# Attention ahead of two Strassen layers: half-row transposes in pairs, and scores copied to SBUF by the maximum

## The chip, the cores and the metric

The kernel runs on one core of a Trainium2 chip. The metric is the device time of one execution in microseconds (us), the median of several. A core has five engines with queues of their own: TensorE (PE, matrix products, with weight loads shown apart as PEld), VectorE (DVE), ScalarE (ACT), GpSimd (POOL) and SyncE (SP), which here issues nearly all DMAs. Each works through its instructions in the order in which the program issues them. PSUM, where TensorE writes, has eight banks of 512 f32 a partition; SBUF is the working memory. A DVE or ACT instruction can read PSUM, POOL reads SBUF alone.

## The reference

Attention with a threshold, for 8 batches and 8 heads of 576 positions and 64 features, all in f32:

```python
scores = scale * np.matmul(q, k.transpose(0, 1, 3, 2))      # scale = 1/8
thresh = np.max(scores, axis=-1, keepdims=True) - tau       # tau = 0.02
scores = np.where(scores >= thresh, scores, -1000000000.0)
scores = scores - np.max(scores, axis=-1, keepdims=True)
attn = np.exp(scores)
attn = attn / (np.sum(attn, axis=-1, keepdims=True) + 1e-09)
return np.matmul(attn, v).astype(np.float32)
```

The result, as 4608 rows of 512, goes through `h = np.maximum(x @ w_in, 0.0)` and `h * h @ w_out`, with a hidden width of 2048.

## The kernel before

The program has two parts. First attention, with the weights of the two layers loaded and prepared beside it; then the two layers as nested Strassen products (`hidden_layer`, `output_layer`), of which nothing is changed but the allocation of their two PSUM buffers.

Two heads make a pair, since two heads of 64 features fill 128 partitions. There are 32 pairs, and 4.5 blocks of 128 queries in each, so 144 *units* of 128 queries by 576 keys for two heads; the fifth unit of a pair is shared with the next. A *period* (`period`, L579) handles two units: A = 2p and B = 2p+1 begin, a and b of the period before are finished, and the values of period m = p-2 are computed. Periods run from -2 to 74. The order in which `period` calls the steps is the program order of every engine; the steps are under a manual schedule, so nothing reorders them.

The steps of a unit:

- `turn`, `turn_last` (L343, L365): q and k of a pair come from DMA with positions on partitions, and are transposed by TensorE, four blocks of 128x128 into one bank of a two-buffer pool; ScalarE copies them out, scaling q by 1/8. The last 64 queries and keys of both heads share one block; POOL copies those keys into block-diagonal tiles (`kdiag`, L376).
- `scores` (L405) multiplies 64x64 parts of q by 512 keys, four products at once on the four quarters of the array; `scores_rest` (L383) gives the last 64 keys of both heads in one 128x128 product with `kdiag`. A score tile has three banks, and there are two of them.
- `softmax` (L420) holds what follows: `top`, VectorE's maximum over both heads from PSUM (L431); `least`, the threshold, on VectorE (L434); `power`, ScalarE's exponential from PSUM (L439); `mask`, VectorE's comparison times the exponential with the row sum accumulated (L444), one per head; `over` on POOL adds 1e-9 (L450); `inverse` on VectorE (L453); `normal`, POOL's scaling by the inverse (L456), one per head.
- `fill` and `filled` (L493, L504) transpose the weights, 18 blocks of 128x128 per period in six fills (two of them in the unused middle of the score tiles, two in the banks of the values), and ScalarE copies each fill to SBUF (L508).
- `values` (L510) multiplies them by v in 64x64 products, 36 per period and 54 where a unit is shared; the result leaves with one of the fills and goes to DRAM by DMA (`give_x`, L537).

Beside this, 32 chunks of the layers' weights come in as 64-bit patterns and are converted in six steps (`convert1` to `convert6`, L198 to L241: two each on ScalarE, POOL and VectorE), one chunk a period from period 2 to 18 and from 33 to 49; two of these steps on VectorE (L225, L233) and all on POOL read only SBUF. Then 88 sums of 128x512 of them (`sums`, L243) and 12 sums of the first x (`prepare_x`, L762) run on POOL (L131, L134), up to three in a period.

Two VectorE instructions of the same form, the mask and the fifth conversion step, as they stand:

```python
nc.vector.scalar_tensor_tensor(                      # L444, of(j) in PSUM
    out=w[:, :, j, :], in0=of(j), scalar=thr[:, j : j + 1], in1=w[:, :, j, :],
    op0=ALU.is_ge, op1=ALU.mult, accum_out=sm[:, j : j + 1],
)
nc.vector.scalar_tensor_tensor(                      # L233, hi and a in SBUF
    out=hi, in0=hi, scalar=-(1 << 30), in1=a, op0=ALU.bitwise_and, op1=ALU.bitwise_or
)
```

Of the kernel before, what the change touches and what calls it, by code (L numbers as in the profile page):

```python
# [48 lines left out]
def kernel(  # L49
# [66 lines left out]
        out=qscale[:, :], in0=tau_c[:, :], scalar1=0.0, scalar2=SCALE, op0=ALU.is_ge, op1=ALU.mult  # L116
# [5 lines left out]

    kdiag = [sb.tile([P, P], FP32, tag=f"kdiag{i}") for i in range(3)]
    qdiag = [sb.tile([P, 2, P], FP32, tag=f"qdiag{i}") for i in range(2)]
    for t in kdiag:
        nc.gpsimd.memset(t[:, :], 0.0)
    for t in qdiag:
        nc.gpsimd.memset(t[:, :, :], 0.0)
# [114 lines left out]
    def sums(W, which, at, done):  # L243

        first = [at[a][b] for a in range(2) for b in range(2)]
        for op, o, x, y in which:
            for k_ in first:
                to = W[o, k_] if o == y else weight_tile(W, o, k_)
                yield op(nc.gpsimd, to[:, :], W[x, k_][:, :], W[y, k_][:, :])
        for m in OUTER:  # L250
            for op, o, x, y in which:
                to = W[m, o] if o == y else weight_tile(W, m, o)
                yield op(nc.gpsimd, to[:, :], W[m, x][:, :], W[m, y][:, :])
            done(m)
# [19 lines left out]
    SPARE = S  # L274
# [24 lines left out]
    def load_k(i):  # L299
# [4 lines left out]
        for j in range(2):  # L304
            queue = nc.scalar if i == 0 and j == 0 else nc.sync
            keys = k[b, h + j, :, :].rearrange("(p c) d -> p c d", c=CH)
            for e in range(2):
                queue.dma_start(
                    out=kn[ds(e * HALF, HALF), :, ds(j * D, D)],
                    in_=keys[:, j : j + CH - 1, :].rearrange("p (t e) d -> p t e d", e=2)[:, :, e, :],  # L310
                )
            queue.dma_start(out=rn[REST:P, ds(j * D, D)], in_=keys[:, 0 if j else CH - 1, :])
# [16 lines left out]
    def places(i):  # L329
        if i not in turned:  # L330
            turned[i] = (
                sb.tile([P, MAIN], FP32, tag="qT", bufs=2, name="qT"),
                sb.tile([P, S], FP32, tag="kT", bufs=3, name="kT"),
            )
# [8 lines left out]
    def turn(i, which):  # L343

        nat, to = loaded.pop((i, which)), places(i)[which]
        pt = bank([P, FULL, P], "pqk")
        for t in range(FULL):
            nc.tensor.transpose(pt[:, t, :], nat[:, t, :], ident[:, :])
        flat, to = pt[:, :, :].rearrange("p t m -> p (t m)"), to[:, 0:MAIN]

        def then():
            if which:
                nc.scalar.copy(to, flat)  # L353
                next_keys(i)
            else:
                nc.scalar.activation(out=to, in_=flat, func=AF.Identity, scale=qscale[:, :])
# [5 lines left out]
    def last_q(i):  # L362
        return qdiag[i // 2 % 2][:, i % 2, :]

    def turn_last(i, pt):  # L365

        rn = loaded.pop((i, 2))
        nc.tensor.transpose(pt, rn[:, :], ident[:, :])

        def then():  # L370
            to = last_q(i)[:, ds(i % 2 * REST, REST)]
            nc.scalar.activation(out=to, in_=pt[:, 0:REST], func=AF.Identity, scale=qscale[:, :])
            nc.scalar.copy(places(i)[1][:, MAIN:S], pt[:, REST:P])
            for j in range(2):
                rows = ds(j * D, D)
                nc.gpsimd.tensor_copy(out=kdiag[i % 3][rows, ds(j * REST, REST)], in_=turned[i][1][rows, MAIN:S])  # L376
# [4 lines left out]
    soft, given = {}, deque()  # L381

    def scores_rest(n, sc):  # L383

        pair, t = units[n]
        to = sc[:, MAIN:S]
        to = bass.AP(tensor=to.tensor, offset=to.offset, ap=[to.ap[0], [2 * BANK - S, 2], [1, REST]])
        if t < FULL:
            nc.tensor.matmul(to, turned[pair[0]][0][:, ts(t, P)], kdiag[pair[0] % 3][:, :], start=True, stop=True)
            return  # L390
        for c, i in enumerate(pair):
            nc.tensor.matmul(to, last_q(i)[:, :], kdiag[i % 3][:, :], start=(c == 0), stop=(c == 1))

    def apart(one, others):

        for o in others:
            tc.declare_no_dep(one.ins, o.ins, reason="other banks")

    mains, middles = {}, {}

    def aside(n, read):
        apart(read, mains.get(n, ()))
        middles.setdefault(n, []).append(read)

    def scores(n, sc):  # L405

        pair, t = units[n]
        mains[n] = []
        for c in range(2):
            for j in range(2):  # L410
                rows, at = ds(j * D, D), ds(c * HALF, HALF)
                qT, kT = turned[pair[c]]
                lhs = qT[rows, ds(t * P + c * HALF, HALF)] if t < FULL else last_q(pair[c])[rows, at]
                made = nc.tensor.matmul(sc[at, ds(j * 2 * BANK, MAIN)], lhs, kT[rows, 0:MAIN], start=True, stop=True)  # L414
                apart(made, middles.get(n, ()))
                mains[n].append(made)

    AT = (0, 2 * BANK - REST)

    def softmax(n, sc):  # L420

        small = sb.tile([P, 4, 2], FP32, tag="small", bufs=4, name="small")
        nmx, thr, sm, rs = (small[:, i, :] for i in range(4))
        both = sc[:, 0:S]
        both = bass.AP(tensor=both.tensor, offset=both.offset, ap=[both.ap[0], [AT[1], 2], [1, S]])
        w = sb.tile([P, CH, 2, D], FP32, tag="w", bufs=4, name="w")
        weights[n] = w
        of = lambda j: sc[:, ds(AT[j], S)].rearrange("p (c d) -> p c d", d=D)

        def top():  # L430
            nc.vector.tensor_reduce(out=nmx, in_=both, axis=AXIS.X, op=ALU.max, negate=True)  # L431

        def least():
            nc.vector.tensor_scalar(  # L434
                out=thr, in0=nmx, scalar1=-1.0, scalar2=tau_p[:, :], op0=ALU.mult, op1=ALU.subtract
            )

        def power(j):
            nc.scalar.activation(  # L439
                out=w[:, :, j, :], in_=of(j), func=AF.Exp, bias=nmx[:, j : j + 1], scale=1.0  # L440
            )

        def mask(j):
            nc.vector.scalar_tensor_tensor(  # L444
                out=w[:, :, j, :], in0=of(j), scalar=thr[:, j : j + 1], in1=w[:, :, j, :],
                op0=ALU.is_ge, op1=ALU.mult, accum_out=sm[:, j : j + 1],
# [30 lines left out]
    class Plan:  # L477


        def __init__(self, m):  # L480
            sizes = (2, 3, 3, 4, 3, 3) if turned_last(m + 2) else (1, 3, 3, 4, 4, 3)
            order = [(u, c) for u in range(2) for c in range(CH)]
            self.fills = [order[sum(sizes[0:f]) : sum(sizes[0 : f + 1])] for f in range(6)]
            self.first = [P if f < 2 else 0 for f in range(6)]
            self.size = [self.first[f] + P * n for f, n in enumerate(sizes)]
            self.base = [sum(self.size[0:f]) for f in range(6)]
            self.at = {
                uc: self.base[f] + self.first[f] + P * i for f, fill in enumerate(self.fills) for i, uc in enumerate(fill)
            }

    plans = {}

    def fill(m, f, pt):  # L493

        if m not in wT:
            wT[m] = sb.tile([P, 5 * BANK], FP32, tag="wT", bufs=1, name="wT")
            plans[m] = Plan(m)
        if has(2 * m):
            for i, (u, c) in enumerate(plans[m].fills[f]):
                w = weights[2 * m + u]  # L500
                to = pt[:, ds(plans[m].first[f] + P * i, P)]
                nc.tensor.transpose(to, w[:, c, :, :].rearrange("p j d -> p (j d)"), ident[:, :])  # L502

    def filled(m, f, pt, pv=False, copy=nc.scalar.copy):  # L504

        plan = plans[m]
        a, z = 0 if pv else plan.first[f], plan.size[f] if has(2 * m) else P
        return copy(wT[m][:, ds(plan.base[f] + a, z - a)], pt[:, a:z])  # L508

    def values(m):  # L510

        out = [bank([P, BANK], f"pv{j}") for j in range(2)]
        x = wT.pop(m)
        for c in range(CH):
            for u in range(2):
                for s, (i, _, count, row) in enumerate(halves(2 * m + u)):
                    for j in range(2):
                        rows = ds(j * D, D)
                        nc.tensor.matmul(  # L519
                            out[j][ds(u * D, D), ds(row, count)], loaded_v[i][rows, c, :],  # L520
                            x[rows, ds(plans[m].at[u, c] + row, count)],
                            start=(c == 0 and s == 0), stop=(c == CH - 1), skip_group_check=True,
                        )
        return out
# [12 lines left out]
    def give_x(m, x, step):  # L537

        for u in range(2):
            rows = ds(u * D, D)  # L540
            for i, first, count, row in halves(2 * m + u):
                b, hp = pairs[i]
                to = xT[b][ds(hp * P, P), ds(first, count)].rearrange("(j d) n -> d j n", j=2)
                of = x[rows, 0 : 2 * step].rearrange("p (j n) -> p j n", j=2)[:, :, ds(row, count)]
                given.append((to, of))
# [5 lines left out]
    OUT_SUMS = 15  # L551
    IN_FIRST = 33
    starts.update({IN_FIRST + m: 16 + m for m in range(16)})
    IN_SUMS = IN_FIRST + 13
    summing = deque()
# [14 lines left out]
    def sums_start(n):  # L570
        if n == OUT_SUMS:
            summing.append(sums(W_OUT, SUMS_B, AT_B, keep))
        if n == IN_SUMS:
            summing.append(sums(W_IN, SUMS_A, AT_A, lambda m: None))

    def begun(n):
        return starts.get(n)

    def period(p):  # L579
# [3 lines left out]
        sc = {}  # L583

        def first(f, pv):
            if has(2 * m) or has(2 * m + 2):
# [580 lines left out]
```

## Time and profile before

| what | us |
|---|---|
| median of three timed runs (1377.78 to 1378.17) | 1378.07 |
| span of the profiled execution, first to last instruction | 1379.4 |
| attention, about 13 to 580 us of the span | 567 |
| TensorE busy in the attention stage | 538 |
| VectorE busy there | 497 |
| ScalarE busy there | 469 |
| POOL busy there | 453 |
| the two layers, from 580 us on | 799 |

The page gives the profiled execution no time but its span. A line of a timeline has the start in us, the duration, the engine, the source line, the operation, what is written and read, and how many such instructions were merged; brackets hold the idle time in front and what ended it. A line of a group has the total busy time and the mean in ns, then the idle time in front of it. A line of a stretch gives its length, then busy us of PE, PEld, DVE, ACT and POOL with the number of instructions in brackets, then the granted TensorE clock as a share of full speed, the busy share of the DMA engines and GB/s. An f32 product shows as two instructions, a transpose as one. [...]

### The profile page before, as it was taken

How to read it: one execution, taken by the hardware profiler on the slowest of the kernel's cores; microseconds unless marked ns; L12 is line 12 of the kernel's file. 1: busy time of each engine (PE TensorE's matmuls, PEld its weight loads, DVE VectorE, ACT ScalarE, POOL GpSimd, SP SyncE). 2: the span in 40 equal slices, each digit the busy share in tenths (PEclk: the TensorE clock that was granted, in tenths of full speed). 3: DMA queues.
4: the chain of work that ended last, by engine and by line, in shares of the span. 5: the costliest groups of instructions: out<-in, count | busy, mean ns of one | idle time of the engine just before them, and what ended most of it. 6: DMA issues, size and time to landing. Idle time of an engine off the chain costs nothing.

```text
span 1379.4 us, 40958 instructions
## 1 busy us (share of the span) xinstructions
PE 1342.9 (97%) x15955; PEld 1185.5 (86%) x15955; DVE 1026.6 (74%) x2136; ACT 861.2 (62%) x1651; POOL 991.7 (72%) x1111
## 2 busy tenths in 40 slices
PE   8999999999999999999999999999999999999998
PEld 5676767666767676799999999999999999999998
DVE  5999988898998888677778777887666456654563
ACT  5999877888987777656766666765733224332330
POOL 2777888898888886355566556656877777777776
PEclk9999999999999999999999999999999999999999
DMA  4454325787432322123432343328962344224411
GB/s 116 129 144 131 93 71 158 215 231 217 135 89 66 75 66 56 36 90 123 151 125 88 106 146 131 110 106 325 386 209 66 116 154 154 85 79 145 154 32 31
DMA packets 200256, 177.26 MB, mean 129 GB/s; under 512 B 95744, under 2 KB 148992, under 8 KB 199168
## 3 DMA queue, kind: packets, MB, share of 16 engines
q1 hardware_dynamic: 198752, 174.24, 40.9%
q8 instruction: 126, 2.06, 0.6%
q10 hardware_dynamic: 1312, 0.41, 0.1%
q14 instruction: 66, 0.54, 0.1%
HBM read 105.12 MB, written 69.47 MB: 127 GB/s over the span
## 4 chain that ended last, share of the span: by engine, by line
PE 54%; DVE 2%; POOL 1%; ACT 1%; issue 1%; DMA 0%; DVEq 0%; POOLq 0%; SPq 0%; ACTq 0%
PE po L948 29%; PE ph L813 25%; DVE arena L134 2%; POOL arena L134 1%; ACT arena L792 0%; ACT arena L725 0%; PE pv L519 0%; DMA wall<-w 0%; POOL arena L456 0%; ACT arena L508 0%; PE pY L502 0%; DVE arena L131 0%; DVEq L134 0%; ACT arena L793 0%; POOLq L134 0%
## 5 line engine op out<-in xcount | busy, mean ns | idle before, releaser
L134 POOL TENSOR_TENSOR arena<-arena 128x512 f32<-128x512 f32 (+1 forms) x314 | 376.9, 1223 | 248.6 <-DVE arena L134 208.8
L813 PE MATMUL ph<-arena,wall 128*128 128x128 f32 x3528 | 396.6, 275 | 1.1 <-DVE arena L134 0.5
L813 PEld LDWEIGHTS ph<-arena,wall 128*128 128x128 f32 x3528 | 394.7, 192 | 2.9 <-DVE arena L134 2.8
L948 PE MATMUL po<-wall,arena 128*128 128x128 f32 x3528 | 396.6, 275 | 0.3
L948 PEld LDWEIGHTS po<-wall,arena 128*128 128x128 f32 x3528 | 394.8, 192 | 2.0 <-issue 1.6
L134 DVE TENSOR_TENSOR arena<-ph,arena 128x512 f32<-128x512 f32 x378 | 255.4, 688 | 92.9 <-PE ph L813 60.3
L431 DVE TENSOR_REDUCE arena<-sc 128x2 f32<-128x1152 f32 x144 | 195.0, 1354 | 52.9 <-PE sc L414 39.3
L134 DVE TENSOR_TENSOR arena<-po,arena 128x128 f32<-128x128 f32 x378 | 107.9, 289 | 169.6 <-PE po L948 168.5
L444 DVE SCALAR_TENSOR_TENSOR arena<-sc,arena 128x576 f32<-128x576 f32 x288 | 222.9, 811 | 14.8 <-ACT arena L439 14.4
L439 ACT ACTIVATE arena<-sc,arena 128x576 f32<-128x576 f32 x288 | 207.3, 750 | 37.4 <-DVE arena L431 32.6
L456 POOL TENSOR_SCALAR arena<-arena 128x576 f32<-128x576 f32 x288 | 214.7, 760 | 19.4 <-DVE arena L453 11.5
L759 ACT COPY c<-arena 128x512 f32<-128x512 f32 (+1 forms) x303 | 172.8, 579 | 62.5 <-DVE arena L131 56.5
L519 PEld LDWEIGHTS pv<-arena 64*64 64x64 f32 x5760 | 151.5, 133 | 40.4 <-issue 22.3
L131 POOL TENSOR_TENSOR arena<-arena 128x512 f32<-128x512 f32 (+1 forms) x138 | 174.7, 1266 | 9.7
L131 DVE TENSOR_TENSOR arena<-arena,c 128x512 f32<-128x512 f32 (+1 forms) x267 | 174.6, 662 | 7.5 <-ACT c L759 6.6
L519 PE MATMUL pv<-arena 64*64 64x128 f32 (+1 forms) x5760 | 157.9, 259 | 0.6 <-ACT arena L353 0.4
L414 PE MATMUL sc<-arena 64*64 64x512 f32 x1152 | 157.4, 617 | 0.0
L792 ACT ACTIVATE arena<-arena 128x512 f32<-128x512 f32 x144 | 89.9, 624 | 76.9 <-POOL arena L134 76.8
L725 ACT COPY arena<-po 128x128 f32<-128x128 f32 x63 | 16.7, 265 | 179.2 <-PE po L948 177.4
L502 PE MATMUL pY<-ident,arena 128*128 128x128 f32 x546 | 86.3, 279 | 27.1 <-ACT arena L508 22.3
L450 POOL TENSOR_SCALAR arena<-arena 128x2 f32<-128x2 f32 x144 | 47.4, 329 | 79.8 <-DVE arena L444 45.3
L502 PEld LDWEIGHTS pY<-ident,arena 128*128 128x128 f32 x546 | 60.3, 141 | 50.6 <-issue 23.9
(67 smaller groups left out, 1259.8 us busy)
## 6 DMA issues: line engine op xcount, KB each, us to landing
g<-arena SPq DMA_DIRECT2D x144, 256.0 KB, 2.0
arena<-g SPq DMA_DIRECT2D x144, 256.0 KB, 4.4
wall<-w SPq DMA_DIRECT2D x49, 256.0 KB, 5.3
arena<-in_v_dram SPq DMA_DIRECT2D x32, 288.0 KB, 3.1
out_dram<-arena SPq DMA_DIRECT2D x70, 128.0 KB, 2.3
arena<-in_q_dram SPq DMA_DIRECT2D x64, 128.0 KB, 3.8
arena<-in_moe_w_out_dram SPq DMA_DIRECT2D x16, 512.0 KB, 4.1
xT<-arena SPq DMA_DIRECT2D x128, 64.0 KB, 2.1
```

The costliest lines, as they stand in the source:

```text
L131: e.tensor_tensor(out=out, in0=x, in1=y, op=ALU.subtract)
L134: e.tensor_tensor(out=out, in0=x, in1=y, op=ALU.add)
L414: made = nc.tensor.matmul(sc[at, ds(j * 2 * BANK, MAIN)], lhs, kT[rows, 0:MAIN], start=True, stop=True)
L431: nc.vector.tensor_reduce(out=nmx, in_=both, axis=AXIS.X, op=ALU.max, negate=True)
L439: nc.scalar.activation(out=w[:, :, j, :], in_=of(j), func=AF.Exp, bias=nmx[:, j : j + 1], scale=1.0)
L444: nc.vector.scalar_tensor_tensor(out=w[:, :, j, :], in0=of(j), scalar=thr[:, j : j + 1], in1=w[:, :, j, :], op0=ALU.is_ge, op1=ALU.mult, a ...
L456: nc.gpsimd.tensor_scalar(out=w[:, :, j, :], in0=w[:, :, j, :], scalar1=rs[:, j : j + 1], scalar2=1.0, op0=ALU.mult, op1=ALU.mult)
L502: nc.tensor.transpose(to, w[:, c, :, :].rearrange("p j d -> p (j d)"), ident[:, :])
L519: nc.tensor.matmul(out[j][ds(u * D, D), ds(row, count)], loaded_v[i][rows, c, :], x[rows, ds(plans[m].at[u, c] + row, count)], start=(c == ...
L759: nc.scalar.copy(c, y)
L813: nc.tensor.matmul(to[:, j, :], W_IN[m, k][:, ts(j, P)], of[k][:, m - 1, :], start=(not more and j == 0), stop=True, skip_group_check=True,)
L948: nc.tensor.matmul(to, g[:, j, :], w[:, j, :], start=(not more and j == 0), stop=(j == 3), skip_group_check=True)
```

## The change

- A 128x128 transpose becomes two of 64 rows by 128 columns (`half_turn`), which write 64 columns each into two banks. This holds for weights, q and k; ScalarE reads them with a pattern that joins the two banks.
- The block-diagonal tails go: the last 64 keys are multiplied in 64x64 parts like the others, and `kdiag`, `qdiag` and their copies on POOL are gone.
- The scores are computed negated. `top` becomes one VectorE pass per head that copies the scores from PSUM to an SBUF tile `s` and accumulates the minimum; `power` and `mask` read `s`. `least` goes to POOL.
- PSUM is cut anew. One score tile of six banks serves all units: A uses banks 0 and 5 with its tails in 1 and 4, B uses banks 2 and 3 with its tails in the same 1 and 4; the values go to 0 and 5, the turns of q and k and one small fill to 2 and 3. The other two banks take the large fills, 8 blocks each, one after the other. `touch` adds a wait between engines that use the same bank and removes those between different banks.
- The weights are transposed in three fills (8, 2 and 8 blocks), the last of which in the next period.
- The steps of a period come in a new order, written out as a list of names; values leave by two small copies of their own.
- The sums of weights are spread: none or one in a period with a conversion, two in the others, the sums of x among them; some sums of W_OUT start earlier.

```diff
     def sums(W, which, at, done):
         first = [at[a][b] for a in range(2) for b in range(2)]
+        def inner(m, kinds):
+            for op, o, x, y in kinds:
+                to = W[m, o] if o == y else weight_tile(W, m, o)
+                yield op(nc.gpsimd, to[:, :], W[m, x][:, :], W[m, y][:, :])
+        early = which[0:3]
+        for m in (1, 2):
+            yield from inner(m, early)
         for op, o, x, y in which:
             for k_ in first:
                 to = W[o, k_] if o == y else weight_tile(W, o, k_)
                 yield op(nc.gpsimd, to[:, :], W[x, k_][:, :], W[y, k_][:, :])
         for m in OUTER:
-            for op, o, x, y in which:
-                to = W[m, o] if o == y else weight_tile(W, m, o)
-                yield op(nc.gpsimd, to[:, :], W[m, x][:, :], W[m, y][:, :])
+            yield from inner(m, which[3:] if m in (1, 2) else which)
             done(m)
...
+    MEET = ({"scores", "turned"}, {"values", "weights"})
+    def touch(what, made, at, size):
+        if at is None:
+            return
+        on = range(at // BANK, (at + size - 1) // BANK + 1)
+        met = {made.ins.engine}
+        for kind, other, others in reversed(touched):
+            e = other.ins.engine
+            if e == made.ins.engine:
+                continue
+            if on[-1] < others[0] or others[-1] < on[0]:
+                if {what, kind} in MEET:
+                    continue
+                tc.declare_no_dep(made.ins, other.ins, reason="other banks")
+            elif e not in met:
+                met.add(e)
+                tc.add_manual_dep(made.ins, other.ins.name, behind, reason="same bank")
+        touched.append((what, made, on))
+        while len(touched) > 300:
+            touched.popleft()
+    def half_turn(pt, slot, of, at=None):
+        for r in range(2):
+            rows = ds(r * HALF, HALF)
+            made = nc.tensor.transpose(pt[:, r, ts(slot, HALF)], of[rows, :], ident[rows, rows])
+            touch("turns", made, at and at + r * BANK, BANK)
+    def whole(pt, slot, count):
+        return pt[:, :, ds(slot * HALF, count * HALF)].rearrange("p r (t q) -> p r t q", q=HALF)
+    def joined(to):
+        return to.rearrange("p (t r q) -> p r t q", r=2, q=HALF)
...
+    def scores(n):
+        of, t = units[n]
+        for at_k, count in ((0, MAIN), (MAIN, REST)):
             for j in range(2):
...
+                first = n % 2 != j
+                to = (3 * j + 2 * first) * BANK if count == MAIN else (3 * j + 1) * BANK + first * (BANK - REST)
+                for c in range(2):
+                    rows, at = ds(j * D, D), ds(c * HALF, HALF)
+                    qT, kT, qR = turned[of[c]]
+                    lhs = qT[rows, ds(t * P + c * HALF, HALF)] if t < FULL else qR[rows, :]
+                    made = nc.tensor.matmul(
+                        sc[at, ds(to, count)], lhs, kT[rows, ds(at_k, count)], start=True, stop=True
+                    )
+                    touch("scores", made, to, count)
...
+        s = sb.tile([P, 2, S], FP32, tag="s", bufs=2, name="s")
...
+        of = lambda j: s[:, j, :].rearrange("p (c d) -> p c d", d=D)
+        def top(j):
+            at = 3 * j * BANK + (n % 2 != j) * (2 * BANK - REST)
+            made = nc.vector.tensor_scalar(
+                out=s[:, j, :], in0=sc[:, ds(at, S)], scalar1=1.0, scalar2=None,
+                op0=ALU.mult, op1=ALU.min, accum_out=nmx[:, j : j + 1],
+            )
+            touch("tops", made, at, S)
         def least():
-            nc.vector.tensor_scalar(
-                out=thr, in0=nmx, scalar1=-1.0, scalar2=tau_p[:, :], op0=ALU.mult, op1=ALU.subtract
-            )
+            nc.gpsimd.tensor_scalar(out=thr, in0=nmx, scalar1=tau_p[:, :], scalar2=None, op0=ALU.add)
         def power(j):
             nc.scalar.activation(
-                out=w[:, :, j, :], in_=of(j), func=AF.Exp, bias=nmx[:, j : j + 1], scale=1.0
+                out=w[:, :, j, :], in_=of(j), func=AF.Exp, bias=nmx[:, j : j + 1], scale=-1.0
             )
         def mask(j):
             nc.vector.scalar_tensor_tensor(
                 out=w[:, :, j, :], in0=of(j), scalar=thr[:, j : j + 1], in1=w[:, :, j, :],
-                op0=ALU.is_ge, op1=ALU.mult, accum_out=sm[:, j : j + 1],
+                op0=ALU.is_le, op1=ALU.mult, accum_out=sm[:, j : j + 1],
             )
...
+    FIRST = [(u, c) for c in range(CH) for u in range(2)]
+    FILLS = {"V": (0, 8), "W": (8, 2), "U": (10, 8)}
...
+            half_turn(pt, i, weights[2 * m + u][:, c, :, :].rearrange("p j d -> p (j d)"), at)
...
+                        made = nc.tensor.matmul(
+                            sc[ds(u * D, D), ds(5 * j * BANK + row, count)], loaded_v[i][rows, (c - (u != j)) % CH, :],
+                            wT[m][rows, ds((2 * c + u) * P + row, count)],
...
+    def sums_due(p):
+        if p < IN_FIRST - 14:
+            return int(p in (7, 8, 9, 11, 12, 13, 15, 16, 17, 18))
+        return 1 if IN_FIRST <= p < IN_FIRST + 17 else 2
...
+    ORDER = """
+        c1 SA overb U eU topA0 powA0 topA1 c3 norma0 SB invb powA1 c4 topB0 norma1
+        leastA normb0 normb1 topB1 maskA0 leastB maskA1 s1 PV powB0 c5 ePV T maskB0 V eT
+        overA powB1 eV W eW c2 maskB1 c6 invA s2 fetch
+    """.split()
...
+            sc = stack.enter_context(tc.tile_pool(name="sc", bufs=1, space=PSUM)).tile([P, 6 * BANK], FP32, name="sc")
+            pt_pool = stack.enter_context(tc.tile_pool(name="pt", bufs=1, space=PSUM))
```

Names in the list: `c1` to `c6` are the conversion steps, `s1` and `s2` the sums, S scores, `U`, `V`, `W` fills and `eU`, `eV`, `eW` their copies, `T` and `eT` the turns, `PV` and `ePV` the values; capital A and B are the units that begin, small a and b those of the period before. A digit is the head.

## The prediction

> **What bounds the kernel now.** First the page's totals, then busy time by stage: attention is the stretch from 13 to 580 us; the two layers behind it are not touched.
>
> ```profile
> span 1379.4 us, 40958 instructions
> PE 1342.9 (97%) x15955; PEld 1185.5 (86%) x15955; DVE 1026.6 (74%) x2136; ACT 861.2 (62%) x1651; POOL 991.7 (72%) x1111
> ```
> ```profile
> 13.00:580.00 567.00, 538.10 (x8762) 386.87 (x8764) 496.91 (x1072) 468.64 (x908) 452.90 (x658) 1.00 0.45 121
> ```
>
> Four engines are at 80 to 95% there. The rows of the reduce line say when a period (two units) begins: 144 reduces start between 13.3 and 568.5 us, so 71.5 steps of two, 7.77 us each. TensorE's timeline through one period shows who sets that:
>
> ```profile
> 534.99 1.09 PE L414 MATMUL sc<-arena 64*64 64x512 f32 x8
> ...
> 538.49 2.15 PE L519 MATMUL pv<-arena 64*64 64x128 f32 x72
> 540.56 0.77 PE L502 MATMUL pv<-ident,arena 128*128 128x128 f32 x5
> 541.71 0.52 PE L502 MATMUL pY<-ident,arena 128*128 128x128 f32 x3 [0.38 <-ACT arena L508]
> ...
> 542.81 1.09 PE L414 MATMUL sc<-arena 64*64 64x512 f32 x8
> ```
>
> From one score step to the same step of the next period (7.82 us) TensorE has one wait worth the name, 0.38 us for an eviction: it sets the pace, with VectorE close behind. The third view is the groups, with the durations used below:
>
> ```profile
> L444 DVE SCALAR_TENSOR_TENSOR arena<-sc,arena 128x576 f32<-128x576 f32 x288 | 222.9, 811 | 14.8 <-ACT arena L439 14.4
> L456 POOL TENSOR_SCALAR arena<-arena 128x576 f32<-128x576 f32 x288 | 214.7, 760 | 19.4 <-DVE arena L453 11.5 <-PE sc L414 1.0
> L431 DVE TENSOR_REDUCE arena<-sc 128x2 f32<-128x1152 f32 x144 | 195.0, 1354 | 52.9 <-PE sc L414 39.3 <-PE sc L389 9.4 <-ACT arena L508 1.1
> L131 POOL TENSOR_TENSOR wall<-wall 128x512 f32<-128x512 f32 x77 | 98.0, 1278 | 2.8
> ```
>
> Last, who holds whom between VectorE and POOL. VectorE's timeline, then POOL's:
>
> ```profile
> 111.10 0.69 DVE L233 SCALAR_TENSOR_TENSOR arena<-arena 128x512 int32<-128x512 int32 x1
> 290.07 1.83 DVE L233 SCALAR_TENSOR_TENSOR arena<-arena 128x512 int32<-128x512 int32 x1
> ```
> ```profile
> 111.13 0.72 POOL L450 TENSOR_SCALAR arena<-arena 128x2 f32<-128x2 f32 x1 [1.18 <-DVE arena L444]
> 290.06 1.28 POOL L131 TENSOR_TENSOR wall<-wall 128x512 f32<-128x512 f32 x1
> 291.44 0.53 POOL L450 TENSOR_SCALAR arena<-arena 128x2 f32<-128x2 f32 x1
> ```
>
> L233 is the only VectorE instruction of this stage with two tensors from SBUF. POOL's little addition, 0.214 us alone, takes 0.72 beside it; L233, 0.69 us alone, takes 1.83 beside a POOL sum of 1.28. They take turns: whoever comes second waits until the other is nearly done. The mask (L444), whose first tensor lies in PSUM, lasts 793 to 819 ns whatever POOL does.
>
> **The change, part by part.**
>
> *Transposes.* In the start-up the old kernel runs both kinds within 3 us at one slow clock:
>
> ```profile
> 4.75 1.09 PE L348 MATMUL pqk<-ident,arena 128*128 128x128 f32 x4
> 6.78 0.53 PE L1009 MATMUL idle<-ident 64*128 64x64 f32 x5
> ```
>
> Taking off one duration (0.42, 0.31), the step is 0.67/3 = 0.22 us for a whole transpose and 0.22/4 = 0.055 for a half-row one, so a pair costs half. At full clock the whole one steps by 0.11 (four in 0.66, one lasting 0.28 to 0.30). Per period 18 transposes of weights and some 4 of q and k: 22 x 0.055 = 1.2 us less TensorE. The tails of scores (128x128 block-diagonal, 0.22 a step) become four small products, 8 instructions at up to 0.03 as in the value products: 0 to 0.1 less per unit. TensorE falls from 7.8 to about 6.5 us a period: it is no longer the bound.
>
> *Maximum.* Two passes of 576 from PSUM with an accumulator instead of one of 1152. Nearest row: the mask, 0.735 us apart back to back. 2 x 0.735 against 1.357: VectorE +0.11 per unit, +0.2 a period. The threshold goes to POOL: VectorE -0.45 a period, POOL +2 x 0.214.
>
> *Mask.* It now reads scores and weights from SBUF: the form of L233. Alone it would last 0.69 to 0.81. But four masks a period now exclude POOL. One 512-wide L233 delays POOL by 0.72 - 0.214 = 0.51 us; for 576 columns 0.57 (above). The case at 290 us, where L233 came second, delayed the POOL addition behind it by some 0.44, for 576 columns 0.50 (below). I take 0.54, the middle of two near ends.
>
> *POOL, now summed.* Per period: 4 scalings at 0.735 (2.94), 2 additions and 2 thresholds at 0.214 (0.86), masks 4 x 0.54 (2.16). A weight sum is 1.28; a conversion 0.61 + 1.04 on POOL and 0.51 + 0.22 of delay by the two VectorE steps of it that read SBUF. The order gives 26 periods a conversion and one sum: 2.94 + 0.86 + 2.16 + 1.28 + 1.65 + 0.73 = 9.6 us. 37 have two sums: 8.5. Six have a conversion alone: 8.3. One has one sum: 7.2. Five at the ends stay as they are. 249.6 + 314.5 + 49.8 + 7.2 = 621 us for 70 periods that now take 70 x 7.77 = 544: **+77 us**. Nothing hides this: each scaling feeds the transposes, and the thresholds, queued behind scalings, feed the masks. The even spread of sums moves work among periods and saves nothing; the 64 copies of keys that go (15.6 us of POOL) are left out of the new sums.
>
> *ScalarE.* Exponentials from SBUF: between 0.68 (the 512-wide SBUF Relu, 0.624, and 64 columns) and the present 0.75. Evictions: 3.16 us a period now; two of 1024 columns (about 1.0 each by the slope from 256 to 512), one of 256, two of 128: 2.9. With turns (0.6) that is 6.4 us, and 7.8 with the two conversion steps (0.72 each): hidden behind POOL's 8.5 and 9.6; with that cover gone it would be next in conversion periods.
>
> *Banks and DMAs.* One score tile in place of two: the next unit's score tails wait for the maximum of this one, which is early in VectorE's queue, ahead of the masks; the middle banks serve turns between maximum and next scores. Behind those waits TensorE has 2 us of slack: 0, at worst 0.4 us a period (the present wait for an eviction), kept for the range. Loads and stores keep their number and queue; issued at other points, they land 2 to 5 us later, with a period of lead.
>
> The sum is made on the profiled span, 1379.4, which is 1.3 us above the median of the timed runs, 1378.07; the page gives that execution no other time. 1378 + 77 = **1455 us**. Its own range: the lower lock price in all masks, 288 x 0.04 = 12 less; masks that fall where POOL waits anyway, at most a third, 50 less; POOL idle 5% of the stage, as it must wait for reciprocals, 30 more; 0.4 x 70 = 28 for banks: 1395 to 1515.
>
> [...]
>
> **Rivals.**
>
> *The mask does not exclude POOL* (float data with an accumulator, contiguous, unlike L233): VectorE binds. Four maxima and four masks at 0.735 and two reciprocals at 0.16 are 6.2 us, conversions 1.1 more, handoffs 0.4: 32 x 7.7 + 38 x 6.6 = 497, so -47: **1331 us**, faster. It speaks for it that L233 is the only witness, against it that all 32 of its rows agree. The price decides: POOL without masks needs 621 - 70 x 2.16 = 470, so below (544 - 470)/280 = 0.26 us of delay per mask the change stops being slower.
>
> [...]
>
> *TensorE's clock falls.* With POOL as the bound TensorE idles 2 to 3 us a period. The clock was granted at 0.5 from 24 us on, after a stretch with little work:
>
> ```profile
> 22.00:24.00 2.00, 0.30 (x4) 0.09 (x2) 2.00 (x4) 1.42 (x4) 1.21 (x2) 0.96 0.41 98
> 24.00:26.00 2.00, 2.00 (x9) 1.73 (x9) 1.90 (x6) 1.43 (x3) 0.21 (x1) 0.50 0.35 67
> ```
>
> At half clock throughout, 5.3 us of streaming would be 10.6 and bind: 70 x 10.6 - 544 = +198, **1576 us**; a busy array gets its clock back, so less. [...]
>
> *Half transposes do not pair*: 1.2 us more TensorE instead of less, 9 us a period, mostly hidden under POOL: 1460 to 1480, within the forecast's range.
>
> **Chances.** Forecast 0.70; mask free of POOL 0.13; half rate 0.05; clock 0.08; something near no change, at 1375 to 1395, 0.04. The range to hold 8 in 10 is the forecast's with part of the clock case: 1395 to 1540. Within 0.2% is what a measurement cannot tell from none: faster 0.14, same 0.02, slower 0.84.
>
> **What would show it.** In the new profile: masks whose durations scatter from 0.75 to nearly 2 us, and scalings on POOL from 0.75 to 1.4; POOL over 90% busy from 30 to 650 us; periods of 9.6, 8.5 and 8.3 us in their stretches; TensorE waiting 2 us a period, mostly for POOL's scalings or VectorE's maxima. [...]

## The result and the profile after

The changed kernel takes **1462.48 us** (median of four runs, 1461.01 to 1466.83), against 1378.12 (1377.78 to 1379.58) for the kernel before: ratio 1.0604, 95% interval 1.058 to 1.0628, 84 us slower. The forecast was 1455.

The head of the page of the changed kernel: span, busy times and TensorE's clock by slices.

```profile
span 1460.6 us, 46093 instructions
PE 1298.7 (89%) x18331; PEld 1140.2 (78%) x18331; DVE 1124.9 (77%) x2424; ACT 876.5 (60%) x1577; POOL 1147.4 (79%) x1186
...
PEclk9999999999899999999999999999999999999999
```

The same by stage (window, its length, then busy time of PE, PEld, DVE, ACT and POOL, clock, DMA share, GB/s); attention now ends at about 661 us and the layers follow.

```profile
13.00:661.00 648.00, 495.17 (x11172) 343.59 (x11174) 593.92 (x1356) 483.16 (x833) 609.71 (x740) 0.97 0.40 106
661.00:1460.60 799.60, 793.91 (x7103) 790.21 (x7094) 529.32 (x1062) 389.33 (x737) 536.85 (x440) 1.00 0.39 134
```

The layers take 800 us as before; the 84 us lie in attention. There POOL is busy 610 of 648 us, 94%, and VectorE 594, which counts the time that its instructions are held. TensorE has fallen to 495.

The costliest groups of the page (instructions of one line, then busy time in all and mean ns of one, then idle time before them and its releaser):

```profile
L461 DVE SCALAR_TENSOR_TENSOR arena<-arena 128x576 f32<-128x576 f32 x288 | 351.0, 1254 | 29.0 <-POOL arena L453 25.5
...
L473 POOL TENSOR_SCALAR arena<-arena 128x576 f32<-128x576 f32 x288 | 253.6, 892 | 6.8
...
L446 DVE TENSOR_SCALAR_CACHE_REDUCE arena<-sc 128x576 f32<-128x576 f32 x288 | 204.7, 746 | 11.1 <-PE sc L428 10.8
```

The mask (L461) takes 1.25 us in the mean. The same line by itself, with the least, median and greatest ns of one, tells why a mean misleads here:

```profile
L461 DVE SCALAR_TENSOR_TENSOR arena<-arena x288: 806/1286/1829, 14.5 to 651.7; 128x576 f32<-128x576 f32 x144
```

The least, 0.806 us, is the mask alone. What lies above it I read as waiting that the profile books as execution. Who holds it is seen by laying the two engines' timelines side by side, in one period with two weight sums. First VectorE (start, duration, instruction, idle time before it), then POOL:

```profile
532.73 0.73 DVE L446 TENSOR_SCALAR_CACHE_REDUCE arena<-sc 128x576 f32<-128x576 f32 x1
...
536.03 1.28 DVE L461 SCALAR_TENSOR_TENSOR arena<-arena 128x576 f32<-128x576 f32 x1 [0.29 <-POOL arena L453]
...
537.25 1.29 DVE L461 SCALAR_TENSOR_TENSOR arena<-arena 128x576 f32<-128x576 f32 x1
...
538.73 1.81 DVE L461 SCALAR_TENSOR_TENSOR arena<-arena 128x576 f32<-128x576 f32 x1 [0.18 <-POOL arena L453]
...
540.47 0.81 DVE L461 SCALAR_TENSOR_TENSOR arena<-arena 128x576 f32<-128x576 f32 x1
...
541.29 0.73 DVE L446 TENSOR_SCALAR_CACHE_REDUCE arena<-sc 128x576 f32<-128x576 f32 x1
```

```profile
535.96 1.97 POOL L473 TENSOR_SCALAR arena<-arena 128x576 f32<-128x576 f32 x2
537.91 0.78 POOL L453 TENSOR_SCALAR arena<-arena,tau_p 128x2 f32<-128x2 f32 x1
538.66 1.27 POOL L124 TENSOR_TENSOR wall<-wall 128x512 f32<-128x512 f32 x1
540.01 0.60 POOL L467 TENSOR_SCALAR arena<-arena 128x2 f32<-128x2 f32 x1
540.69 1.72 POOL L124 TENSOR_TENSOR wall<-wall 128x512 f32<-128x512 f32 x1
```

From one first maximum (532.73) to the next (541.29) is the period: 8.56 us. POOL's five lines follow each other with gaps of at most 0.08 us. The third mask (538.73, 1.81 us) starts just after the sum (538.66, 1.27) and ends at 540.54, some 0.6 us after the sum's end; the addition that follows on POOL is held in turn and ends at 540.61, with the mask. That addition of two numbers per partition (L467, 0.60 us) and the threshold (L453, 0.78) are nearly three times as long as undisturbed (0.214 and 0.29). Neither engine idles much, and both lose.

Over the whole stage, POOL's stretching is the busy time of each group less its count times its undisturbed duration (0.75 for a scaling; 0.29 for the threshold, as in the kernel with a one-tensor mask below; 0.214 for the addition):

```profile
L124 POOL TENSOR_TENSOR wall<-wall 128x512 f32<-128x512 f32 x77 | 110.7, 1437 | 2.2
...
L453 POOL TENSOR_SCALAR arena<-arena,tau_p 128x2 f32<-128x2 f32 x144 | 94.1, 653 | 14.8 <-DVE arena L446 13.5 <-DVE arena L470 1.4
...
L467 POOL TENSOR_SCALAR arena<-arena 128x2 f32<-128x2 f32 x144 | 60.3, 419 | 17.4 <-DVE arena L470 3.2 <-DVE arena L461 2.0
```

Scalings 253.6 - 216 = 38, thresholds 94.1 - 41.8 = 52, additions 60.3 - 30.8 = 30, sums 110.7 - 98.6 = 12 (1.28 each), the last conversion step (L234, 32 of them in 47.5 us, 1.04 each alone) 14: 146 us. That would be 0.51 us for each of 288 masks, but not all of it is theirs: the conversion's two-tensor step takes a part (a threshold at 402.97 us lasts 1.31 us, behind a mask and then that step at 403.53). The kernel with a one-tensor mask, below, gives 0.46 to 0.48 a mask.

### The profile page after: what moved, and what is told of

The parts are those of the page before. It is cut to its first block, busy times and chain, and to the rows that moved or that the text cites. A ratio compares the mean times of both kernels' runs of the same rounds, so it can differ in the third digit from the quotient of the medians.

```text
span 1460.6 us, 46093 instructions
## 1 busy us (share of the span) xinstructions
PE 1298.7 (89%) x18331; PEld 1140.2 (78%) x18331; DVE 1124.9 (77%) x2424; ACT 876.5 (60%) x1577; POOL 1147.4 (79%) x1186
## 4 chain that ended last, share of the span: by engine, by line
PE 50%; ACT 1%; DVE 1%; POOL 1%; issue 1%; DMA 1%; DVEq 0%; POOLq 0%; SPq 0%; ACTq 0%
PE po L913 27%; PE ph L778 22%; DVE arena L127 1%; POOL arena L127 1%; ACT arena L757 1%; ACT arena L690 0%; DMA g<-arena 0%; ACT arena L758 0%; PE sc L517 0%; DMA wall<-w 0%; POOL arena L473 0%; PE pt L373 0%; ACT c L724 0%; ACT arena L508 0%; DVE arena L124 0%
## 5 line engine op out<-in xcount | busy, mean ns | idle before, releaser
L461 DVE SCALAR_TENSOR_TENSOR arena<-arena 128x576 f32<-128x576 f32 x288 | 351.0, 1254 | 29.0 <-POOL arena L453 25.5
L428 PE MATMUL sc<-arena 64*64 64x512 f32 (+1 forms) x2304 | 220.2, 445 | 60.8 <-DVE arena L446 58.9
L473 POOL TENSOR_SCALAR arena<-arena 128x576 f32<-128x576 f32 x288 | 253.6, 892 | 6.8
L456 ACT ACTIVATE arena<-arena 128x576 f32<-128x576 f32 x288 | 216.3, 777 | 61.3 <-DVE arena L446 56.5
L428 PEld LDWEIGHTS sc<-arena 64*64 64x64 f32 x2304 | 84.0, 138 | 187.3 <-DVE arena L446 128.1
L446 DVE TENSOR_SCALAR_CACHE_REDUCE arena<-sc 128x576 f32<-128x576 f32 x288 | 204.7, 746 | 11.1 <-PE sc L428 10.8
L373 PE MATMUL pt<-ident,arena 64*128 64x64 f32 x2304 | 120.0, 236 | 90.3 <-POOL arena L473 87.8
L508 ACT COPY arena<-pt 128x1024 f32<-128x1024 f32 x144 | 146.0, 1014 | 75.9 <-PE pt L373 74.1
L373 PEld LDWEIGHTS pt<-ident,arena 64*128 64x128 f32 x2304 | 93.4, 144 | 107.2 <-POOL arena L473 97.7
L517 PE MATMUL sc<-arena 64*64 64x128 f32 (+1 forms) x5760 | 167.4, 262 | 0.0
L517 PEld LDWEIGHTS sc<-arena 64*64 64x64 f32 x5760 | 151.5, 134 | 0.2
```

The lines of the kernel that those rows point to most:

```text
L373: made = nc.tensor.transpose(pt[:, r, ts(slot, HALF)], of[rows, :], ident[rows, rows])
L428: made = nc.tensor.matmul(sc[at, ds(to, count)], lhs, kT[rows, ds(at_k, count)], start=True, stop=True)
L446: made = nc.vector.tensor_scalar(out=s[:, j, :], in0=sc[:, ds(at, S)], scalar1=1.0, scalar2=None, op0=ALU.mult, op1=ALU.min, accum_out=nmx ...
L456: nc.scalar.activation(out=w[:, :, j, :], in_=of(j), func=AF.Exp, bias=nmx[:, j : j + 1], scale=-1.0)
L461: nc.vector.scalar_tensor_tensor(out=w[:, :, j, :], in0=of(j), scalar=thr[:, j : j + 1], in1=w[:, :, j, :], op0=ALU.is_le, op1=ALU.mult, a ...
L473: nc.gpsimd.tensor_scalar(out=w[:, :, j, :], in0=w[:, :, j, :], scalar1=rs[:, j : j + 1], scalar2=1.0, op0=ALU.mult, op1=ALU.mult)
```

## Experiments

Theory: a mask with two SBUF inputs and a POOL instruction that reads SBUF shut each other out; POOL is the longest queue, so its delay sets the period. Rivals: the copying maximum, the half-row transposes, the shared banks, the clock, or POOL's load without any exclusion.

**A mask with one SBUF tensor.** The comparison alone is written, and its row sum accumulated; the multiplication by the exponentials is left out.

```diff
-nc.vector.scalar_tensor_tensor(out=w[:, :, j, :], in0=of(j), scalar=thr[:, j : j + 1],
-    in1=w[:, :, j, :], op0=ALU.is_le, op1=ALU.mult, accum_out=sm[:, j : j + 1])
+nc.vector.tensor_scalar(out=w[:, :, j, :], in0=of(j), scalar1=thr[:, j : j + 1],
+    scalar2=None, op0=ALU.is_le, op1=ALU.add, accum_out=sm[:, j : j + 1])
```

> The changed kernel, but the mask is a comparison of the scores in SBUF with the threshold, with the row sum accumulated: one tensor from SBUF in place of two. Left out: the multiplication by the exponentials, which ScalarE still computes. Exclusion theory: masks steady near 0.75 us beside POOL, scalings and sums on POOL at 0.75 and 1.28, periods of 6.7 us with two sums and 7.6 with a conversion, about 1331 us (1315 to 1360). Rival, that the single score tile and its bank waits set the pace (TensorE waits 187 us for the maxima): periods stay near 8.5, 1440 to 1465 us.

Measured: 1346.1 us, ratio 0.9751 (0.9734 to 0.9768) to the kernel before. The mask and the scaling in its source-line and group views, then the stage:

```profile
L461 DVE TENSOR_SCALAR_CACHE_REDUCE arena<-arena x288: 787/808/836, 15.8 to 537.4; 128x576 f32<-128x576 f32 x144
```

```profile
L473 POOL TENSOR_SCALAR arena<-arena 128x576 f32<-128x576 f32 x288 | 216.8, 766 | 6.9
```

```profile
13.00:545.00 532.00, 472.00 (x11102) 341.55 (x11096) 484.27 (x1360) 463.55 (x833) 471.20 (x740) 0.99 0.48 129
```

All 288 masks now last 0.79 to 0.84 us, the scaling falls from 0.892 to 0.766, and POOL's busy time from 610 to 471, near the 470 that the prediction's rival gave it without masks. This form, a tensor and a multiplication less, is worth 1462.5 - 1346.1 = 116 us. It lasts as long as the old mask from PSUM (0.808 us against 0.811), so all that the change does besides is worth about 1346.1 - 1378.1 = -32 us, a gain.

The two kernels also give the price of a mask. Here is the stretch of one period with two sums, of the changed kernel and then of this one:

```profile
532.73:541.29 8.56, 6.65 (x152) 4.59 (x148) 8.04 (x20) 6.25 (x11) 8.21 (x11) 1.00 0.32 70
```

```profile
431.38:437.95 6.57, 6.18 (x148) 4.62 (x148) 6.02 (x19) 5.94 (x12) 6.21 (x11) 1.00 0.32 70
```

In the mean of 35 such periods POOL is busy 8.19 us and 6.33 us: 1.86 us for four masks, 0.46 each. Over the stage it is (609.7 - 471.2)/288 = 0.48.

**The exclusion brought into the kernel before**, in two runs that differ by one operand of the mask (and by the signs that go with it, in the threshold and the comparison). Both give the kernel before a copying maximum and the exponential from the copy; the first has the mask read the copy too, the second leaves the mask on PSUM.

```diff
-nc.vector.tensor_reduce(out=nmx, in_=both, axis=AXIS.X, op=ALU.max, negate=True)
+for j in range(2):
+    nc.vector.tensor_scalar(out=s[:, j, :], in0=sc[:, ds(AT[j], S)], scalar1=-1.0,
+        scalar2=None, op0=ALU.mult, op1=ALU.min, accum_out=nmx[:, j : j + 1])
...
-    ..., in_=of(j), func=AF.Exp, bias=nmx[:, j : j + 1], scale=1.0
+    ..., in_=of_s(j), func=AF.Exp, bias=nmx[:, j : j + 1], scale=-1.0
...
-    ..., in0=of(j), ..., op0=ALU.is_ge, op1=ALU.mult     # from here on the first of the two runs only
+    ..., in0=of_s(j), ..., op0=ALU.is_le, op1=ALU.mult
...
-    out=thr, in0=nmx, scalar1=-1.0, scalar2=tau_p[:, :], op0=ALU.mult, op1=ALU.subtract
+    out=thr, in0=nmx, scalar1=1.0, scalar2=tau_p[:, :], op0=ALU.mult, op1=ALU.add
```

> The kernel before, with its banks, order, transposes and sums, but the maximum is two passes that copy the negated scores to SBUF, and exponential and mask read the copy. Exclusion theory: masks scatter between 0.8 and 1.9 us, POOL is stretched by 140 to 160 us, 1440 to 1500 us. Rival, that the new order, banks and fills cost the time and the mask's source does not: 1375 to 1400 us.

> As the kernel before with the copying maximum, exponential from the copy, but the mask still reads its scores from PSUM. Exclusion theory: masks steady at 0.81 us, two passes of some 0.68 in place of one of 1.36, so within 1% of before: 1370 to 1395 us. Rival, that the copying pass itself (another write to SBUF beside POOL) slows the stage: over 1420 us, near the run with the mask from SBUF.

Measured: 1474.16 us, ratio 1.067 (1.0647 to 1.0692), with the mask from SBUF; 1380.65, ratio 1.0012 (0.9996 to 1.0027), with the mask from PSUM. Mask and weight sum in the groups of the first:

```profile
L450 DVE SCALAR_TENSOR_TENSOR arena<-arena 128x576 f32<-128x576 f32 x288 | 317.0, 1136 | 4.2
...
L131 POOL TENSOR_TENSOR wall<-wall 128x512 f32<-128x512 f32 x77 | 128.0, 1667 | 2.8
```

and of the second:

```profile
L450 DVE SCALAR_TENSOR_TENSOR arena<-sc,arena 128x576 f32<-128x576 f32 x288 | 223.4, 813 | 4.2
...
L131 POOL TENSOR_TENSOR wall<-wall 128x512 f32<-128x512 f32 x77 | 98.0, 1279 | 2.8
```

Same instruction, same size, first operand `sc,arena` or `arena`: the mask goes from 0.813 to 1.136 us, the sum from 1.279 to 1.667, the kernel by 93.5 us. The copying maximum by itself costs nothing there. So it is the second SBUF operand and neither the multiplication nor the copy.

**Half of the masks.** The one-tensor form for the first head only (for it, the multiplication is left out).

> The changed kernel with the one-tensor mask for the first head of each unit only (its multiplication by the exponentials left out), the other head's mask as changed: two masks a period with two tensors from SBUF instead of four. Exclusion theory: half the delays go, 2 x 0.54 us a period: periods of 7.5 us with two sums and 8.7 with a conversion and a sum, 1385 to 1405 us. Rival, that what the one-tensor run gained came from another thing than the number of excluding masks: no place between 1346 and 1462 us is forecast.

Measured: 1398.8 us (1396.64 to 1402.0), periods of 7.62 us with two sums and 8.84 with a conversion and a sum (medians). The masks that still read two tensors stay stretched:

```profile
L467 DVE SCALAR_TENSOR_TENSOR arena<-arena 128x576 f32<-128x576 f32 x144 | 164.4, 1142 | 0.1
```

From all masks to half 64 us go, from half to none 53: the price goes roughly with the number of such masks, 0.44 and 0.37 us of the kernel's time for each.

**Fewer sums.** The changed kernel with its sums of weights and x moved behind attention; W_OUT's sums then read places that W_IN has already taken, so that part is computed from other data.

> The changed kernel with the 100 POOL sums moved behind attention, where POOL does them alone (some 125 us, with the layers waiting). Exclusion theory, with POOL and the masks as one shared resource: periods without a conversion fall from 8.56 to 6.6 to 7.2 us, those with a conversion from 9.78 to the 8.77 of the present ones without a sum; in all 1450 to 1500 us. Rival, that the banks or the order set the pace: periods stay at 8.5 and 9.8, and the whole rises to some 1585 us.

Measured in a single run: 1486.22 us. Periods without a conversion fall from 8.56 to 6.70 us in the median (6.45 to 7.41), those with one from 9.78 to 8.76. The stage, and the stretch behind it in which the sums are done:

```profile
13.00:570.00 557.00, 481.17 (x11208) 346.74 (x11207) 497.58 (x1356) 469.35 (x835) 459.27 (x645) 0.96 0.40 100
570.00:700.00 130.00, 22.37 (x152) 21.40 (x151) 9.19 (x14) 6.58 (x12) 120.56 (x99) 0.56 0.29 112
```

Exclusion alone does not make a period long: with 459 us of POOL work in 557 (82%) there is room for it. Without the sums such a period takes 6.70 us, with two sums but without exclusion (the one-tensor mask) 6.61, with both 8.56. Exclusion decides because POOL also carries the sums. Uncovered, they take a stretch of 130 us, more than the 91 by which attention ends earlier.

**Whole transposes in the changed kernel.**

```diff
-for r in range(2):
-    rows = ds(r * HALF, HALF)
-    made = nc.tensor.transpose(pt[:, r, ts(slot, HALF)], of[rows, :], ident[rows, rows])
...
+flat = pt.rearrange("p r n -> p (r n)")
+made = nc.tensor.transpose(flat[:, ts(slot, P)], of, ident[:, :])
...
```

> The changed kernel with whole 128x128 transposes in place of the paired half rows, into the same two banks. TensorE has some 1.2 us more a period. Exclusion theory (VectorE and POOL taking turns set the pace, TensorE waits over 2 us a period): hidden, 1462 to 1485 us, periods of 8.56 and 9.78 us grow by less than 0.3. Rival, that TensorE is still on the path: 70 x 1.2 = 84 more, near 1545 us.

Measured: 1461.71 us (1461.41 to 1462.86), the same as with halves. TensorE's busy time differs as meant, 547 us here against 495, and its clock too, 0.99 against 0.97:

```profile
13.00:661.00 648.00, 547.10 (x9625) 391.57 (x9625) 592.10 (x1354) 477.07 (x832) 607.44 (x739) 0.99 0.40 106
```

The halves' 52 us less of TensorE change nothing, and neither does the lower clock that came with them.

**Paired halves alone in the kernel before**, for the four or five weight blocks that go into the two banks of the values:

```diff
-nc.tensor.transpose(...)                    # block by block, one bank after the other
+for r in range(2):
+    rows = ds(r * HALF, HALF)
+    nc.tensor.transpose(pts[r][:, ds(P + HALF * i, HALF)], w[rows, :], ident[rows, rows])
...                                          # the values read the halves from their new places
```

> The kernel before with one part of the change alone: the four or five blocks of weights that go to the two banks of the values are transposed by paired half rows (the other 13 or 14 blocks stay whole; mask from PSUM, order, banks and sums as before). TensorE has 4.6 x 0.055 = 0.25 us less a period. If TensorE sets the pace of the kernel before, 70 x 0.25 = 17 less: 1360 to 1370 us, and never slower. Rival, that VectorE with 95% in conversion periods holds the pace there: only the other 38 periods gain, 1367 to 1375 us; or nothing, 1375 to 1382, if handoffs between fills and evictions hold it.

Measured: 1391.2 us, ratio 1.0089 (1.0075 to 1.0103), a miss. TensorE has less to do, but its timeline shows that it now waits:

```profile
548.31 0.52 PE L504 MATMUL pv<-ident,arena 64*128 64x64 f32 x10
...
549.59 0.52 PE L526 MATMUL pY<-ident,arena 128*128 128x128 f32 x3 [0.76 <-ACT arena L532]
```

Its waits for the copy out of those banks, of this kernel and then of the kernel before (us in all, times, longest):

```profile
PE pY L526 <- ACT arena L532: 43.2, 59, 1.0
```

```profile
PE pY L502 <- ACT arena L508: 19.7, 59, 1.0
```

Halves fill two banks at once, so neither can be copied before the last block: in the kernel before, ScalarE's first copy of a fill starts at 541.08 us while the transposes run on to 541.33; here one starts at 556.82, behind their end at 556.74. The five pairs take 0.52 us where five whole blocks took 0.77, and the wait behind them grows from 0.38 to 0.76. From the first of these transposes to the next fill it takes 0.97 us with four whole blocks and 1.19 with five (means), 1.17 and 1.30 with pairs. That is 0.20 and 0.11 more, some 11 us over 70 periods, which is most of the 13 us of loss. As far as this run shows, then, the pace of the kernel before is a loop from TensorE through ScalarE's copies and back, and TensorE's stream is only part of it.

**Two attempts at a faster kernel.** The first takes the small instructions off POOL: the threshold goes to ScalarE, and the addition of 1e-9 is left out. The second also has ScalarE scale one of a period's four weight tiles. In both the list of steps is changed to match: the additions go, and the thresholds come elsewhere.

```diff
-nc.gpsimd.tensor_scalar(out=thr, in0=nmx, scalar1=tau_p[:, :], scalar2=None, op0=ALU.add)
+nc.scalar.activation(out=thr, in_=nmx, func=AF.Identity, bias=tau_p[:, :], scale=1.0)
...
+if (n % 2, j) in [(1, 1)]:                  # the second only
+    nc.scalar.activation(out=w[:, :, j, :], in_=w[:, :, j, :], func=AF.Identity, scale=rs[:, j : j + 1])
+    return
```

> The changed kernel with its POOL relieved of small work: the addition of 1e-9 to the row sums is left out (each is at least 1, so it has no effect in f32), and the threshold is computed by ScalarE. Exclusion theory: 4 x 0.25 us less POOL a period, 1395 to 1415 us. Rival, that VectorE's own queue with its waits sets the pace whatever POOL's small work: 1450 us or more.

> The same, and one of the four scalings of a period is done by ScalarE: 0.73 us less POOL a period. Exclusion theory: periods near 7.0 us with two sums and 8.1 with a conversion and a sum, 1340 to 1375 us, faster than the kernel before although the masks still read two tensors from SBUF. Rival: ScalarE becomes the bound in conversion periods (7.3 us a period of work now, 0.7 more), above 1380 us.

Measured: 1423.67 us, ratio 1.032 (1.0302 to 1.0338), periods of 8.0 and 9.08; and 1391.38, ratio 1.0085 (1.0062 to 1.0108), periods of 7.53 and 8.38. Better than the changed kernel, but less than expected both times. A stretch without conversions of the first kernel, then of the second; then two masks of the second and the two POOL sums beside them:

```profile
460.00:600.00 140.00, 118.95 (x2764) 82.27 (x2764) 140.00 (x313) 113.29 (x226) 111.95 (x107) 1.00 0.27 61
```

```profile
460.00:570.00 110.00, 97.10 (x2316) 69.20 (x2310) 110.00 (x261) 100.61 (x205) 75.07 (x72) 1.00 0.30 69
```

```profile
505.46 1.54 DVE L461 SCALAR_TENSOR_TENSOR arena<-arena 128x576 f32<-128x576 f32 x1
...
506.93 1.81 DVE L461 SCALAR_TENSOR_TENSOR arena<-arena 128x576 f32<-128x576 f32 x1
```

```profile
505.10 3.03 POOL L124 TENSOR_TENSOR wall<-wall 128x512 f32<-128x512 f32 x2
```

VectorE now has no gap in 140 and 110 us, while POOL idles for a fifth and then a third. The second's masks stand 1.5 and 1.8 us because they wait for two sums (3.03 us on POOL from 505.10). I had priced the exclusion on POOL's queue alone; relieve POOL, and VectorE pays. In the second kernel's conversion periods (320 to 415 us) VectorE is busy 90.9 of 95 us and ScalarE 89.5, so the rival that ScalarE becomes the bound there isn't excluded. No kernel here that computes the whole reference beats the one before. A changed kernel whose mask reads PSUM again was not tried.

## Why the prediction was right

- **The mask as the form of L233: right.** Every sign that it named is there: durations from 0.81 to 1.83 us, scalings stretched, POOL at 94%. The price of 0.54 us per mask, taken from 32 conversion steps, measured 0.46 to 0.48, below even the lower end of 0.50. The break-even of the rival without exclusion (0.26 us) was clearly passed. That rival's 1331 us is what the kernel with a one-tensor mask came near to: 1346.
- **POOL, now summed: right, with two errors that nearly cancel.** Periods of 9.6, 8.5 and 8.3 us were forecast; the means measured are 9.70, 8.54 and 8.69: 26 x 0.10 + 37 x 0.04 + 6 x 0.39 = 6 of the 7 us by which the sum fell short (77 against 84). Inside a period with two sums the forecast had 2.94 + 0.86 + 2.56 = 6.36 us of POOL's own work and 2.16 of delay. The one-tensor mask's kernel shows 6.33 of work, so the work was right. The delay measured 1.86, 0.30 less than forecast. The remaining 0.35 of the 8.54 us are small gaps between POOL's instructions, which the sum put at nothing and only its range allowed for. That the two made up for each other, and the period came out to 0.04, is luck.
- **"Each mask delays POOL" was only half of the mechanism.** The delays were summed on POOL, the longer queue, so the total holds. That VectorE is held as well (masks of up to 1.83 us against 0.806) and can become the bound (no gap in 140 us of the first attempt) was not in the working, and it spoiled the forecasts of both attempts.
- **Masks at half rate (chance 0.05): not seen.** The fastest mask takes 0.806 us, as with one operand in PSUM (0.813, mean), and the conversion step without accumulator (L226) 0.683 us for 512 columns in the changed kernel; no run shows the form at half that rate. For the exclusion itself the evidence is the pair of runs that differ in one operand: 0.813 against 1.136 us a mask and 1380.65 against 1474.16 us in all. By what means the two engines hold each other up, no trace shows.
- **Half-row transposes: pairing right, size and role wrong.** 16 halves in the changed kernel, and 8 whole blocks in the one with whole transposes:

```profile
539.83 0.72 PE L373 MATMUL pt<-ident,arena 64*128 64x64 f32 x16
```

```profile
537.31 1.09 PE L372 MATMUL pt<-ident,arena 128*128 128x128 f32 x8
```

  The records overlap, 16 of 0.23 us in 0.72. With one's length (0.23 and 0.28) taken off, a further pair takes (0.72 - 0.23)/7 = 0.07 us, not 0.055, against 0.12 for a whole block. The 0.055 came from the start-up, where a whole block took 0.22 us; its granted clock reads 1.00 from 4 to 8 us, so that a slow clock was the reason is not shown. TensorE gains 52/70 = 0.74 us a period, not 1.2. All of it is hidden, as the forecast said of anything under POOL's sum.
- **TensorE "sets the pace" before: too simple.** Less TensorE work in the value banks made the kernel before slower, since a wait for ScalarE's copy took its place.
- **Maximum and ScalarE: near.** Two passes are 0.68 apart, not 0.735. The exponential from SBUF takes 0.777 us, above the range of 0.68 to 0.75; the wide evictions 1.014, as said. Both stay hidden.
- **Banks: in range, as far as seen.** No run separates their cost. In the stage's waits (who for whom, us in all, times, longest), TensorE's weight loads stand 127 us behind the maxima for score banks and 98 behind POOL's scalings. The products themselves leave 648 - 495 = 153 us free there, so this is the idleness of an engine that does not bind:

```profile
PEld sc L428 <- DVE arena L446: 127.3, 137, 2.0
PEld pt L373 <- POOL arena L473: 97.7, 71, 1.9
```

- **The clock: fell, but not as a bound.** It was 0.97 in the stage, and the whole-block kernel at 0.99 took the same time. The fall came in eleven stretches of some 3.4 us at 0.50, as from 395.0 to 398.3 us, though no gap in TensorE's work in the stage is longer than 1.8 us. In the kernel before, too, TensorE had stood no longer than 1.70 us before the 0.50 from 24 us on, and its clock was back at 1.00 from 28 us. So the prediction did well to keep this case, though half clock throughout did not come.

## What to carry to other kernels

Count the SBUF operands of every VectorE instruction that runs beside GpSimd work on SBUF: here a second one made the two engines take turns, at 0.46 to 0.48 us of POOL's time for each 576-column instruction. The price fell on the longer of the two queues, so moving work off one showed the other: in the first attempt, with POOL busy 112 of 140 us, VectorE had no gap. A faster form for an engine that did not set the period bought nothing (1462.48 us with halves, 1461.71 with whole blocks), and where it finished two buffers together in place of one after the other, it cost time (1391.2 us, ratio 1.0089).

## What the runs showed of the hardware unexpectedly

- The one-tensor comparison with accumulator, SBUF to SBUF in f32, takes 0.808 us for 576 columns (median of 288) and leaves POOL nearly alone (scalings at 0.766 in the mean, conversion steps included).
- ScalarE's exponential of 576 columns is slower from SBUF (0.777 us in the changed kernel) than from PSUM (0.750 in the kernel before); in the kernel before with the copy alone it takes 0.778.
- A POOL instruction on 128x2 takes 0.29 us with its scalar read from a tile (the threshold, median in the kernel with a one-tensor mask) and 0.214 with a constant (the addition, median in the kernel before).
